# Attention, a leaky-ReLU FFN and a gated FFN in one kernel: the list scheduler's DMA model is given other rates, latencies and a limit on transfers in flight

## The chip, the cores and the metric

The kernel runs on one core of one Trainium2 chip. The metric is the time of one execution in device microseconds (us); the median of three executions stands for a kernel. The engines of the core are PE (TensorE: matmuls, and its weight loads, PEld), DVE (VectorE), ACT (ScalarE), POOL (GpSimd) and SP (SyncE), which here only issues DMAs. Each engine runs its own instructions in program order and waits on semaphores for the others.

## The reference

Three stages follow one another; `x` is what goes from one to the next.

```python
# attention: 4 batches, 8 heads, S = 576, D = 64
scores = q @ k.T / sqrt(64)
cum    = cumsum(log(clip(f, 1e-4, 1)))            # along S, per head
scores = where(causal, -1e9, scores + cum[:, None] - cum[None, :])
attn   = softmax(scores)
x      = (attn @ v)      -> [2304 tokens, 512]
# FFN 1: 512 -> 2048 -> 512
h = x @ w_in;  g = maximum(0.01 * h, h);  x = g @ w_out
# FFN 2: 512 -> 1024 -> 512
h = x @ w2_in; solu = h * softmax(h)
ln = (solu - mean(solu)) / sqrt(var(solu) + 1e-6) * g_ln
out = ln @ w2_out
```

## The kernel before, in words

**Arithmetic.** Where fp32 accuracy is wanted, an operand is split into a high and a low half (a copy, L427/L430/L434, and a subtraction, L442, or L438 where a scale goes with it), and a matmul is three matmuls: high by high, high by low, low by high. So every weight chunk and every block of tokens costs copies and subtractions on ACT, DVE and POOL before PE can use it.

**Attention** goes by 16 pairs of heads. For a pair, pass A does query blocks 0 and 1 and pass B blocks 2 to 4; PASSES (L43) lists eight groups of four pairs, A0, A1, B0, A2, B1, A3, B2, B3 (the figure is the batch). A group needs q and k in SBUF: for pass A `raw<-kqa` and four small rows `raw<-dr_d` that carry the decay, for pass B `raw<-kq`, split into `kq` tiles by copies and subtractions on any of ACT, DVE and POOL; V is loaded as `vr<-vt` and split into `VT`. PE writes scores into `ps_s`, DVE masks them and takes the row maximum (L707), ACT takes the exponential (L657), ACT and DVE scale the result into fp16 halves `hl` (L427, L438), a DMA transpose `pt<-hl` (L470, issued by SP) turns them, PE multiplies by V into `ps_v`, ACT and DVE write that to `xr` (L739, L742), and a DMA spills it to memory: `xs_d<-xr`. There are four `pt` buffers and three `hl` buffers.

**FFN 1, first half.** Nine of the 16 chunks of both weight matrices, wi0 to wi8 and wo0 to wo8, are loaded in 18 transfers of 512 KB each (`wst<-wa`) through three staging buffers, wst0 to wst2. For each, a copy on ACT or POOL makes `wk` from it, DVE shifts bits in place (L812), a copy on ACT, DVE or POOL makes the high half, and a subtraction on POOL or DVE (L442, `wi<-wst,wi` or `wo<-wst,wo`) the low half; then the staging buffer is free for the next transfer. The staging buffers stand in the same memory as the x and g tiles of the FFN, and an operation of no cost frees these only when the last of the 18 is done, so the first FFN matmul waits for all 18. Then the blocks of 256 tokens follow in the order 0, 1, 4, 2, 5, 3, 6, 7, 8 (ORDER), while attention goes on: block 4 is the second block of batch 0 and needs the spill of group B0. A block loads x (`sd<-xs_d`), splits it (`x<-sd`, `x<-sd,x`), multiplies (`ps_f<-x,wi`, "hid" below: 12 matmuls a chunk), applies the leaky ReLU (L853 to L855), multiplies by the second matrix (`ps_f<-g,wo`, "y" below) and spills a partial y to `yp_d`.

**Second phase.** When attention is over, the other seven chunks of both matrices and FFN 2's weights come in through `raw`, and each block of tokens finishes FFN 1 and runs FFN 2 (`ph`, softmax, layer norm, transpose `tr<-hl`, and `py` for the output).

**What sets the order.** Nothing of the above is issued at once. Each piece is recorded as an operation with a duration, a priority, the buffers that it reads and writes and the engines that may do it (class Plan). Plan.run (L161) then plays the program through with a model of the machine: each free engine takes the operation of smallest priority whose inputs have arrived in the model and whose buffers are free in it, and calls its `emit` at that moment. An operation with several engines (flex, L441 to L446 for copies and subtractions) goes to the one where the model sees it done first. So the model's times decide three things and no more: the order of the instructions on each engine, the engine of a flexible operation, and which physical buffer it gets. All DMAs are issued by SP, in the order of the model. In the model a DMA operation is made in move (L462) or turn (L469, transposes), with `dma=` as its time on the transfer engines, which it passes through one after another; in run it has an issue time, a time `ready` at which it may use them, and `end`, at which what depends on it may start. The old model also holds SP during a transpose until the transfer engines are free.

Of the kernel before, what the change touches and what calls it, by code (L numbers as in the profile page):

```python
# [94 lines left out]
WEIGHT2 = {"DVE": 2.58}  # L95
KEPT = {13: (5000.0, -1), 14: (5001.0, -1), 15: (5002.0, -1)}
HEAT = 0.25
TOPE = 267.42
QUEUES = ("SP",)
SHARE = 0.62  # L100
# [11 lines left out]
class Plan:  # L112
# [50 lines left out]
    def run(self):  # L163
# [2 lines left out]
        pool = {e: [] for e in engines}  # L166
        events, cnt = [], 0
        dma_free = hw_free = 0.0
        left = len(self.ops)
        warm, win, busy = False, 0, 0.0  # L170

        def push(t, kind, x):
            nonlocal cnt
            cnt += 1
            heapq.heappush(events, (t, cnt, kind, x))
# [68 lines left out]
        now = 0.0  # L244
        while left:
            moved = True
            while moved:
                moved = False
                for e in engines:
                    if free_at[e] > now or not pool[e]:  # L250
                        continue
                    skipped, got = [], None
                    while pool[e]:
                        item = heapq.heappop(pool[e])
                        o = item[2]
                        if o.taken:
                            continue
                        if o.dma is not None and o.prio > URGENT and dma_free - now > BACKLOG:
                            push(dma_free - BACKLOG + 1.0, 0, None)
                            skipped.append(item)  # L260
                            continue
                        if can_alloc(o) and not (isinstance(o.eng, tuple) and better_elsewhere(o, e)):
                            got = o
                            break
                        skipped.append(item)
                        if len(skipped) > 60:
                            break
                    for item in skipped:
                        heapq.heappush(pool[e], item)
                    if got is None:  # L270
                        continue
                    o = got
                    if isinstance(o.eng, tuple):
                        o.dur, o.eng = cost(o, e), e
                    o.taken = True
                    for b in sorted((b for b in o.bufs if b.slot is None), key=lambda b: b.seq):
                        b.slot = b.tag.free.pop(0)
                        b.t = b.slot() if callable(b.slot) else b.slot
                        b.tag.head += 1
                        bequeath(b.tag)  # L280
                    o.emit()
                    left -= 1
                    moved = True
                    hold = o.dur
                    if e == "PE":
                        hold = pe_time(hold, now, o.heat)
                    elif o.dma is not None and e != "POOL":
                        at = max(now, hw_free)
                        hw_free = at + 460.0
                        hold += at - now  # L290
                    if o.dma is not None:
                        turns = hold >= 1175.0 and e == "SP"
                        ready = (at + (625.0 if turns else 460.0) if e != "POOL" else now + hold) + 650.0
                        s = max(dma_free, ready)
                        if turns:
                            hold += s - ready
                        dma_free = s + o.dma
                        end = dma_free + 1000.0
                    else:
                        end = now + hold + LAT.get(e, 0.0)  # L300
                    free_at[e] = now + hold
                    push(now + hold, 0, None)
                    push(end, 1, o)
                    push(end + TOPE, 2, o)
            if not left:
                break
            assert events, "stuck: " + str([(e, len(p), p[0][:2] if p else None) for e, p in pool.items()])
            now, _, kind, o = heapq.heappop(events)
# [49 lines left out]
def body(tc, kqa, kq, vt, f, wa, w2i, w2o, gln, out):  # L358
    nc = tc.nc
    es = ExitStack()  # L360
    P = Plan()
    PE, ACT, DVE, POOL, SP, CTL = "PE", "ACT", "DVE", "POOL", "SP", "CTL"
# [81 lines left out]
    def flex(engs, durs, emit, prio, **kw):  # L444
        box = []
        o = P.op(tuple(engs) if len(engs) > 1 else engs[0], tuple(durs) if len(engs) > 1 else durs[0],  # L446
                 lambda: emit(box[0].eng), prio, **kw)
        box.append(o)
        return o
# [10 lines left out]
    queue = {SP: nc.sync, ACT: nc.scalar, POOL: nc.gpsimd}  # L460

    def move(dst, src, nbytes, prio, engs=QUEUES, **kw):  # L462
        d = {SP: 475.0, ACT: 490.0, POOL: 1040.0}
        return flex(engs, [d[e] for e in engs], lambda e: queue[e].dma_start(dst(), src()), prio, dma=nbytes / 360.0, **kw)

    def load(buf, dst, src, nbytes, prio, mode="w", **kw):
        return move(dst, src, nbytes, prio, **{mode: [buf]}, **kw)

    def turn(dst, src, n, prio, **kw):  # L469
        return P.op(SP, max(350.0 + 0.875 * n, 1175.0), lambda: nc.sync.dma_start_transpose(out=dst(), in_=src()), prio, dma=0.875 * n, **kw)  # L470

    def mm(o, l, r, start, stop):
        nc.tensor.matmul(o, lhsT=l, rhs=r, start=start, stop=stop)  # L473
# [671 lines left out]
```

## Time and profile before

| | |
|---|---|
| median of 3 executions | 849.26 us (847.44 to 851.11) |
| the profiled execution | 848.65 us |
| its span, first to last instruction | 846.9 us |
| PE busy | 767.9 us, 91% |
| DVE, ACT, POOL busy | 519.4, 490.1, 348.8 us |
| DMA queue of SP | 107.35 MB, 52.3% of the transfer engines' time |

The span leaves 1.75 us of the execution's time outside. The table by stretches (windows) says for each stretch from:to, in us from the span's start, its length, then the busy time of PE, PEld, DVE, ACT and POOL with the instructions in brackets, then the mean granted clock of PE as a share of full speed, the share of the transfer engines' time and the GB/s that they moved. A row of a timeline is one instruction or a run of equal ones: start, length, engine, line, operation, what it writes and from what, shape, count, and in square brackets the idle time before it and what ended that. A row of the waits says which PE instruction waited for which instruction of another engine: total, times, longest.

### The profile page before, as it was taken

What the parts mean: (1) busy time and instruction counts of PE and PEld (TensorE: products, weight loads), DVE (VectorE), ACT (ScalarE), POOL (GpSimd) and SP (SyncE); (2) the same over time, 40 slices, a digit from 0 to 9 for tenths busy, and PEclk for the clock granted to TensorE, in tenths of its full rate; (3) what the DMA queues carried; (4) which work ended last, traced back from release to release, by engine and by line L of the source; (5) the groups of instructions that cost most, each with busy time, mean ns of one, the idle gap of its engine ahead of it and who ended that gap; (6) DMA issues with size and microseconds to landing.
All of it is one profiled execution on the core that took longest, in us unless ns stands there. A gap on an engine that the chain in (4) does not pass through costs nothing.

```text
span 846.9 us, 16019 instructions
## 1 busy us (share of the span) xinstructions
PE 767.9 (91%) x5648; PEld 695.5 (82%) x5648; DVE 519.4 (61%) x1350; ACT 490.1 (58%) x1242; POOL 348.8 (41%) x448
## 2 busy tenths in 40 slices
PE   1753798979999999999899998999999999999996
PEld 1432698968998999999899987898889988998885
DVE  5788767888888878884654667334633434253551
ACT  4886768889889889884555543232333243333321
POOL 6648545166618564822610443422332233222321
PEclk9999999989999999999999999999999999999999
DMA  8997457687789677694655643321332131312223
GB/s 230 220 223 245 96 130 151 150 221 154 136 162 216 155 163 151 174 160 148 195 172 177 189 104 104 71 79 16 98 71 68 26 87 38 87 26 63 26 56 82
DMA packets 184402, 108.37 MB, mean 128 GB/s; under 512 B 150033, under 2 KB 167137, under 8 KB 184321
## 3 DMA queue, kind: packets, MB, share of 16 engines
q1 hardware_dynamic: 184320, 107.35, 52.3%
q8 instruction: 44, 0.72, 0.4%
q14 instruction: 38, 0.30, 0.1%
HBM read 57.39 MB, written 14.78 MB: 85 GB/s over the span
## 4 chain that ended last, share of the span: by engine, by line
PE 64%; DMA 10%; DVE 9%; ACT 8%; issue 4%; POOL 3%; SPq 0%; ACTq 0%; DVEq 0%; POOLq 0%
PE ps_f L473 40%; PE ph L473 10%; PE py L473 6%; PE ps_s L473 5%; PE ps_v L473 3%; ACT ps_s L657 2%; DMA raw<-w2o 2%; DMA tr<-hl 2%; DMA raw<-kq 2%; DMA wst<-wa 1%; DMA pt<-hl 1%; ACT hl L427 1%; DVE hl L438 1%; DMA qa<-sd 1%; DVE ps_s L707 1%
## 5 line engine op out<-in xcount | busy, mean ns | idle before, releaser
L473 PE MATMUL ps_f<-x,wi 128*128 128x256 f32 x972 | 131.7, 289 | 1.2 <-POOL x L442 1.1
L473 PE MATMUL ps_f<-g,wo 128*128 128x256 f32 x972 | 126.4, 284 | 2.5 <-DVE g L855 2.5
L473 PEld LDWEIGHTS ps_f<-x,wi 128*128 128x128 f32 x972 | 124.7, 193 | 3.1 <-POOL x L442 1.9
L473 PEld LDWEIGHTS ps_f<-g,wo 128*128 128x128 f32 x972 | 120.8, 188 | 4.0 <-DVE g L855 2.9
L473 PE MATMUL ph<-wi,g 128*128 128x512 f32 x408 | 98.5, 397 | 1.4 <-DVE raw L968 1.4
L473 PE MATMUL ps_f<-x,wib 128*128 128x256 f32 x756 | 97.3, 279 | 1.8 <-DVE g L855 1.7
L438 DVE SCALAR_TENSOR_TENSOR hl<-ps_s,st,hl 128x512 f16<-128x512 f32 (+4 forms) x160 | 82.8, 540 | 19.4 <-ACT hl L427 16.5
L473 PEld LDWEIGHTS ps_f<-x,wib 128*128 128x128 f32 x756 | 91.6, 188 | 2.9 <-DVE g L855 2.8
L473 PEld LDWEIGHTS ph<-wi,g 128*128 128x128 f32 x408 | 75.9, 188 | 19.3 <-DVE raw L968 1.6
L855 DVE TENSOR_TENSOR g<-ps_f,g 128x256 fp32r<-128x256 f32 x144 | 60.3, 420 | 48.1 <-ACT ps_f L854 47.2
L853 ACT ACTIVATE g<-ps_f 128x256 fp32r<-128x256 f32 x144 | 54.8, 380 | 59.3 <-PE ps_f L473 58.1
L657 ACT ACTIVATE ps_s<-ps_s,st 128x512 f32<-128x512 f32 (+4 forms) x160 | 78.6, 491 | 10.1 <-DVE st L707 6.1
L473 PE MATMUL ps_f<-wo,x 128*128 128x512 f32 x348 | 84.0, 396 | 0.0
L427 ACT ACTIVATE hl<-ps_s,st 128x512 f16<-128x512 f32 (+4 forms) x151 | 76.1, 532 | 11.6 <-DMA pt<-hl 4.7
L473 PE MATMUL ps_v<-pt,VT 128*128 128x128 f16 (+1 forms) x928 | 62.3, 220 | 20.0 <-DVE xr L742 9.0
L473 PE MATMUL py<-g,wob 128*128 128x256 f32 x567 | 75.6, 278 | 2.0 <-ACT g L427 2.0
L473 PEld LDWEIGHTS ps_f<-wo,x 128*128 128x128 f32 x348 | 64.8, 188 | 15.1
L473 PE MATMUL ps_s<-kq 128*128 128x512 f32 (+5 forms) x256 | 66.7, 380 | 11.6 <-DVE hl L438 5.5
L442 POOL TENSOR_TENSOR kq<-raw,kq 64x576 fp32r<-64x576 f32 (+1 forms) x53 | 67.9, 1283 | 21.5 <-ACT kq L427 15.2
L473 PEld LDWEIGHTS <-VT 128*128 128x128 f16 x928 | 50.0, 102 | 30.4 <-issue 15.4
L473 PEld LDWEIGHTS py<-g,wob 128*128 128x128 f32 x567 | 71.2, 188 | 4.3 <-ACT g L427 2.3
L707 DVE CUSTOM_DVE_ANT_0 ps_s<-ps_s,mask 128x256 f32<-128x256 f32 (+3 forms) x128 | 62.2, 496 | 5.9 <-PE ps_s L473 4.5
(159 smaller groups left out, 1221.7 us busy)
## 6 DMA issues: line engine op xcount, KB each, us to landing
wst<-wa SPq DMA_DIRECT2D x18, 512.0 KB
sd<-xs_d SPq DMA_DIRECT2D x32, 256.0 KB
raw<-kq SPq DMA_DIRECT2D x16, 480.0 KB
raw<-wa SPq DMA_DIRECT2D x14, 512.0 KB
raw<-yp_d SPq DMA_DIRECT2D x18, 256.0 KB
vr<-vt SPq DMA_DIRECT2D x13, 320.0 KB
raw<-w2i SPq DMA_DIRECT2D x8, 512.0 KB
raw<-w2o SPq DMA_DIRECT2D x8, 512.0 KB
```

The lines of the kernel that those rows point to most:

```text
L427: nc.scalar.activation(o, i, CP, scale=1.0 if scale is None else scale)
L438: nc.vector.scalar_tensor_tensor(o, a, scale, b, op0=ALU.mult, op1=ALU.subtract)
L442: (nc.vector if eng == DVE else nc.gpsimd).tensor_tensor(o, a, b, op=ALU.subtract)
L473: nc.tensor.matmul(o, lhsT=l, rhs=r, start=start, stop=stop)
L657: P.op(ACT, act(W, 1, True) + 93, lambda view=view, j=j, k=k: nc.scalar.activation(view(), view(), AF.Exp, bias=sts.t[:, j:j + 1], scale=- ...
L707: P.op(DVE, dve(W) + 130, lambda i=i, j=j, view=view: nc.vector.tensor_tensor_reduce(view(), view(), mask[:, 512 - 128 * i:640], -0.125, 3 ...
L853: P.op(ACT, act(n, 0, True), lambda: nc.scalar.activation(g.t[:, 0, 0:n], h(), AF.Prelu, scale=WSC, alpha=0.01), eprio, w=[(g, 0)], r=[ps])
L855: P.op(DVE, dve(n) + 60, lambda: nc.vector.tensor_tensor(g.t[:, 1, 0:n], h(), g.t[:, 0, 0:n].bitcast(F32), op=ALU.subtract), eprio, w=[(g, ...
```

## The change

Only the scheduler's model of DMA differs. A transfer's time in the model goes from its bytes over 360 to its bytes over 267 per ns, so 512 KB take 1.96 us instead of 1.46; a transpose of n columns takes 1.28 n ns instead of 0.875 n. SP is no longer held during a transpose. `ready` is 1300 ns (transposes) or 900 ns after the issue, `end` 700 ns after the transfer, and an issue waits in the model for the landing of the eighth one before it (LANES). The instructions themselves, their shapes and their number of bytes stay; what moves is their order, some choices of engine and some buffers.

```diff
+LANES = 8
@@ run
+        lands = []
@@
-                        at = max(now, hw_free)
+                        at = max(now, hw_free, lands[-LANES] if len(lands) >= LANES else 0.0)
                         hw_free = at + 460.0
                         hold += at - now
                     if o.dma is not None:
-                        turns = hold >= 1175.0 and e == "SP"
-                        ready = (at + (625.0 if turns else 460.0) if e != "POOL" else now + hold) + 650.0
-                        s = max(dma_free, ready)
-                        if turns:
-                            hold += s - ready
-                        dma_free = s + o.dma
-                        end = dma_free + 1000.0
+                        ready = at + (1300.0 if o.dur >= 1175.0 else 900.0) if e != "POOL" else now + hold + 650.0
+                        dma_free = max(dma_free, ready) + o.dma
+                        end = dma_free + 700.0
+                        if e != "POOL":
+                            lands.append(end)
@@ move
-  dma=nbytes / 360.0
+  dma=nbytes / 267.0
@@ turn
-  dma=0.875 * n
+  dma=1.28 * n
```

The first place is SP's queue while the last weights are loaded, before the FFN's first matmul. `pt<-hl` are transposes of group A1, `wst2` is the staging buffer that carries wo4 and then wi8, and `raw0<-kq`, `raw1<-kq` start group B0. Before:

```order
L470 DMA_TRANSPOSE pt1_138<-hl0_134 128x6x128
L470 DMA_TRANSPOSE pt2_139<-hl1_135 128x6x128
L464 DMA wst2_160<-wa 128x2048
L464 DMA wst0_158<-wa 128x2048
L464 DMA raw2_83<-dr_d_104 4x256
L470 DMA_TRANSPOSE pt3_140<-hl2_136 128x6x128
L464 DMA xs_d0_91<-xr1_142 128x256
L464 DMA wst1_159<-wa 128x2048
L464 DMA raw2_83<-dr_d_104 4x256
L464 DMA raw0_81<-kq 128x960
L464 DMA kq1_1_152<-dr_d_104 4x960
L464 DMA raw1_82<-kq 128x960
```

After, from the transpose that stands one ahead of these:

```order
L470 DMA_TRANSPOSE pt0_137<-hl2_136 128x6x128
L464 DMA wst2_160<-wa 128x2048
L464 DMA raw1_82<-dr_d_104 4x256
L470 DMA_TRANSPOSE pt1_138<-hl0_134 128x6x128
L464 DMA xs_d0_91<-xr0_141 128x256
L464 DMA raw1_82<-dr_d_104 4x256 x2
L464 DMA raw2_83<-kqa 64x2x512
L464 DMA wst0_158<-wa 128x2048
L464 DMA raw2_83<-dr_d_104 4x256
L470 DMA_TRANSPOSE pt2_139<-hl1_135 128x6x128
```

The load of wo4 into wst2 moves ahead of two transposes, `pt1<-hl0` and `pt2<-hl1`, and that of wi7 into wst0 ahead of one; a little later, wi8's load into wst2 stands directly behind wo5's into wst1, ahead of both `raw<-kq`, where it was behind them.

The second place is POOL in the same stretch, from wo5's subtraction to wo6's; `kq` are the split q and k of B0's first pairs. Before:

```order
L434 TENSOR_SCALAR kq1_0_151<-raw0_81 64x960
L442 TENSOR_TENSOR kq1_1_152<-raw0_81,kq1_0_151 64x576
L442 TENSOR_TENSOR wo5_77<-wst1_159,wo5_77 128x512
L442 TENSOR_TENSOR kq0_1_150<-raw0_81,kq0_0_149 64x576
L434 TENSOR_SCALAR kq2_0_153<-raw1_82 64x960
L442 TENSOR_TENSOR kq2_1_154<-raw1_82,kq2_0_153 64x576
L442 TENSOR_TENSOR wi8_71<-wst2_160,wi8_71 128x512
```

After:

```order
L442 TENSOR_TENSOR wo5_77<-wst1_159,wo5_77 128x512
L434 TENSOR_SCALAR kq0_0_149<-raw0_81 64x960
L442 TENSOR_TENSOR wi8_71<-wst2_160,wi8_71 128x512
L671 TENSOR_SCALAR st1_129<-st1_129 128x2
L442 TENSOR_TENSOR kq0_1_150<-raw0_81,kq0_0_149 64x576
```

Five pieces of `kq` stood ahead of wi8's subtraction, and one does now; the others come behind it, or go to another engine.

The third place is SP's queue where FFN block 4 is to start: `xs_d0<-xr1` with 320 columns is the last spill of group B0, `sd1` and `sd0<-xs_d0` load block 4's x, and the transposes are those of group A2. Before:

```order
L470 DMA_TRANSPOSE pt1_138<-hl1_135 128x6x128
L464 DMA raw2_83<-kq 128x960
L470 DMA_TRANSPOSE pt2_139<-hl2_136 128x6x128
L470 DMA_TRANSPOSE pt3_140<-hl0_134 128x6x128
L464 DMA yp_d1_96<-yo0_736 128x256
L464 DMA xs_d0_91<-xr1_142 128x320
L464 DMA raw0_81<-kq 128x960
L464 DMA vr0_108<-vt 128x640
L464 DMA yp_d1_96<-yo1_737 128x256
L464 DMA raw1_82<-kq 128x960
L464 DMA sd1_85<-xs_d0_91 128x2x256
L464 DMA sd0_84<-xs_d0_91 128x2x256
```

After:

```order
L464 DMA raw2_83<-kq 128x960
L464 DMA yp_d1_96<-sd2_86 128x256
L464 DMA vr0_108<-vt 128x640
L464 DMA xs_d0_91<-xr1_142 128x320
L470 DMA_TRANSPOSE pt2_139<-hl2_136 128x6x128
L464 DMA raw0_81<-kq 128x960
L470 DMA_TRANSPOSE pt3_140<-hl0_134 128x6x128
L464 DMA yp_d1_96<-yo0_739 128x256
L464 DMA sd1_85<-xs_d0_91 128x2x256
L464 DMA sd0_84<-xs_d0_91 128x2x256
L464 DMA xs_d2_93<-xr0_141 128x256
L464 DMA raw1_82<-kq 128x960
```

The spill stood behind two transposes and a `yp_d` and now stands ahead of them; the loads of x come ahead of `raw1<-kq` and of one `yp_d`. On PE the last matmuls of B0 (`ps_v<-pt,VT`) now have 54 y matmuls of FFN block 1 left behind them, where they had 30.

Elsewhere the same model moves instructions in most of the program. Among the flexible operations, `x<-sd` subtractions on DVE go from 24 to 34 and on POOL from 48 to 38; the copies `kq<-raw` on ACT from 12 to 6 and on POOL from 20 to 26.

## Rows read from the trace of the kernel before

**Rows 1.** The page: span, and busy time, share and instructions by engine.

```profile
span 846.9 us, 16019 instructions
PE 767.9 (91%) x5648; PEld 695.5 (82%) x5648; DVE 519.4 (61%) x1350; ACT 490.1 (58%) x1242; POOL 348.8 (41%) x448
```

**Rows 2.** Stretches of the span (columns as told above).

```profile
64.00:85.00 21.00, 8.07 (x21) 4.84 (x22) 17.94 (x42) 13.71 (x29) 17.11 (x14) 1.00 0.69 238
...
134.00:179.00 45.00, 43.66 (x424) 41.83 (x425) 34.72 (x129) 39.78 (x116) 18.42 (x25) 1.00 0.68 155
179.00:196.00 17.00, 11.10 (x54) 8.29 (x53) 14.94 (x45) 14.83 (x42) 12.97 (x15) 0.70 0.78 219
...
240.00:381.00 141.00, 138.39 (x1287) 130.72 (x1286) 117.33 (x378) 125.85 (x353) 77.38 (x97) 1.00 0.79 170
...
478.00:550.00 72.00, 67.47 (x404) 58.85 (x403) 44.59 (x79) 28.00 (x58) 29.39 (x38) 1.00 0.41 107
550.00:804.00 254.00, 253.32 (x1633) 227.49 (x1632) 107.92 (x207) 85.56 (x190) 73.60 (x109) 1.00 0.24 57
804.00:847.00 43.00, 36.28 (x153) 28.04 (x151) 14.81 (x24) 10.11 (x17) 8.54 (x14) 0.99 0.30 68
```

**Rows 3.** Timeline of PE, around the FFN's first matmuls.

```profile
84.14 0.82 PE L473 MATMUL ps_v<-pt,VT 128*128 128x128 f16 x6 [5.71 <-DVE VT L438]
...
92.41 1.41 PE L473 MATMUL ps_f<-x,wi 128*128 128x256 f32 x5
```

**Rows 4.** Timeline of SP, the loads through wst2 and what is ahead.

```profile
51.06 5.53 SPq L470 DMA_TRANSPOSE pt<-hl  x3
56.69 1.00 SPq L464 DMA_DIRECT2D wst<-wa  x2
...
65.85 0.35 SPq L464 DMA_DIRECT2D wst<-wa  x1
...
79.11 0.33 SPq L464 DMA_DIRECT2D wst<-wa  x1
```

**Rows 5.** Timeline of POOL in the same stretch.

```profile
48.85 1.29 POOL L442 TENSOR_TENSOR wi<-wst,wi 128x512 fp32r<-128x512 f32 x1
...
67.16 1.31 POOL L434 TENSOR_SCALAR kq<-raw 64x960 fp32r<-64x960 f32 x1
...
74.33 1.58 POOL L442 TENSOR_TENSOR kq<-raw,kq 64x576 fp32r<-64x576 f32 x1
77.25 1.83 POOL L442 TENSOR_TENSOR wi<-wst,wi 128x512 fp32r<-128x512 f32 x1 [1.34 <-ACT wi L427]
...
86.55 1.29 POOL L442 TENSOR_TENSOR wo<-wst,wo 128x512 fp32r<-128x512 f32 x1 [1.32 <-ACT wo L427]
```

**Rows 6.** One stretch of 4 us in the same place.

```profile
76.00:80.00 4.00, 2.04 (x5) 0.95 (x3) 3.92 (x9) 3.44 (x9) 2.75 (x2) 1.00 0.32 108
```

**Rows 7.** Timeline of PE: the last matmuls of group B0.

```profile
171.66 0.95 PE L473 MATMUL ps_v<-pt,VT 128*128 128x128 f16 x14
```

**Rows 8.** Timeline of SP, from B0's spill to block 4's x.

```profile
174.13 2.56 SPq L470 DMA_TRANSPOSE pt<-hl  x2
...
177.36 0.44 SPq L464 DMA_DIRECT2D xs_d<-xr  x1
...
180.67 0.96 SPq L464 DMA_DIRECT2D sd<-xs_d  x2
```

**Rows 9.** Timeline of PE: a wait before block 4, and its first matmuls.

```profile
182.98 0.49 PE L473 MATMUL ps_v<-pt,VT 128*128 128x128 f16 x6 [3.53 <-DVE xr L742]
...
189.55 3.35 PE L473 MATMUL ps_f<-x,wi 128*128 128x256 f32 x11 [1.12 <-POOL x L442]
```

**Rows 10.** PE's waits, 196 to 480 us: the longest.

```profile
PE ps_f L473 <- DVE g L855: 2.3, 1, 2.3
```

**Rows 11.** Timeline of DVE: one shape, without and beside POOL's subtraction.

```profile
68.45 0.55 DVE L442 TENSOR_TENSOR kq<-raw,kq 64x384 fp32r<-64x384 f32 x1
...
79.13 1.61 DVE L442 TENSOR_TENSOR kq<-raw,kq 64x384 fp32r<-64x384 f32 x1
```

More of the change, by code (lines that the diff above doesn't have):

```diff
@@ L463, in move @@
         d = {SP: 475.0, ACT: 490.0, POOL: 1040.0}
-        return flex(engs, [d[e] for e in engs], lambda e: queue[e].dma_start(dst(), src()), prio, dma=nbytes / 360.0, **kw)
+        return flex(engs, [d[e] for e in engs], lambda e: queue[e].dma_start(dst(), src()), prio, dma=nbytes / 267.0, **kw)
     def load(buf, dst, src, nbytes, prio, mode="w", **kw):
@@ L469, in turn @@
     def turn(dst, src, n, prio, **kw):
-        return P.op(SP, max(350.0 + 0.875 * n, 1175.0), lambda: nc.sync.dma_start_transpose(out=dst(), in_=src()), prio, dma=0.875 * n, **kw)
+        return P.op(SP, max(350.0 + 0.875 * n, 1175.0), lambda: nc.sync.dma_start_transpose(out=dst(), in_=src()), prio, dma=1.28 * n, **kw)
     def mm(o, l, r, start, stop):
```

## The prediction, made before the changed kernel ran

> **What bounds the kernel now.** I read the page's busy times first. PE works 767.9 us of a span of 846.9 [rows 1], so the whole span holds 79 us in which PE does nothing, and no other engine comes near it. The change alters the order of instructions and some choices of engine; PE's matmuls stay, so the time can move only as those 79 us move, or as the granted clock makes the same matmuls longer.
>
> Second, the table by stretches, to see where they lie [rows 2]. A stretch's length less PE's busy time is its idle time: 5.9 us of 17 in 179 to 196, 4.5 us of 72 in 478 to 550, 6.7 us of 43 at the end, 2.6 us of 141 in 240 to 381, and 0.7 us of 254 in 550 to 804. The greatest part is ahead of the FFN: of 64 to 85 PE works only 8.07 us, and the timeline of PE shows its first FFN matmul at 92.41 [rows 3]. From 134 on PE is full but for a single hole, 179 to 196, and there its granted clock is 0.70 on the mean of the stretch, between the two levels of 2.4 and 1.2 GHz, after PE had little to do.
>
> Third, the timelines around those two places, to see which wait ends last.
>
> **The start.** The first FFN matmul needs all 18 weight chunks through three staging buffers. The loads through wst2 form the chain. Its buffer came free when POOL's subtraction for wi5 ended at 48.85 + 1.29 = 50.14 [rows 5], but SP issued the next load into it, wo4, in the pair at 56.69, since three transposes held SP from 51.06 for 5.53 us [rows 4]. wi8 followed at 65.85 and wo8 at 79.11 [rows 4]. From wo4 to wi8 is 9.2 us, from wi8 to wo8 13.3 us, and from wo8 to the end of its subtraction 86.55 + 1.29 − 79.11 = 8.7 us [rows 4, 5]; 4.6 us later the FFN starts. The middle turn is the long one, because POOL did `kq` pieces from 67.16 to 74.33 + 1.58 = 75.91 and only then wi8's subtraction at 77.25 [rows 5].
>
> **The hole.** The last matmuls of group B0 are issued at 171.66 [rows 7]. Their spill `xs_d<-xr` leaves only at 177.36: two transposes held SP from 174.13 for 2.56 us ahead of it, and block 4's x is loaded at 180.67, 3.3 us after the spill [rows 8]. PE's first full run of matmuls on that x begins at 189.55 [rows 9].
>
> **The change, part by part.** No instruction is removed or added that weighs on PE. The parts of the model (rates, latencies, SP no longer held, eight in flight) act only through one order, so I price the order where PE waits, and not each constant.
>
> *wo4 ahead of two transposes.* One transpose of the three costs SP 5.53 / 3 = 1.84 us [rows 4]. With two behind it and one before, the pair's first load is issued at about 51.06 + 1.84 = 52.9 instead of 56.69: −3.8 us. The two transposes are late by one issue and by one load's time on the transfer engines. Who waits for them? Their products are multiplied by V of group A1, and PE's first matmuls of that kind stand at 84.14, held for 5.71 us by VT and not by the transposes [rows 3]. So this delay is covered by some 25 us; if the cover were gone, it would cost the 3.7 us of two transposes.
>
> *wi8's subtraction ahead of four `kq` pieces.* Five pieces on POOL come to 1.31 + 1.70 + 1.51 + 0.98 + 1.58 = 7.1 us between 67.16 and 75.91 (the first and the last are shown, [rows 5]); one stays ahead. At most 5.8 us go from wi8's turn. But something else is late next: the transfer engines. From 76 to 80 they are busy at 0.32 [rows 6], because there wo8 still waits for its buffer, so 0.68 × 4 = 2.7 us of that stretch stand empty; the page's slices before it show them nearly full. With the loads ahead of it unchanged in bytes, wo8 can move into those 2.7 us and little further, though its buffer would be free 3.8 + 5.8 us earlier. The pieces of `kq` behind wi8 belong to group B0, whose first scores PE does before 84 but whose matmuls by V stand behind block 0's hid in PE's order, so they have cover too.
> Between 2.7 and the 3.8 of wo4's own issue, and since the 0.69 of 64 to 85 [rows 2] leaves a little room more, I take −3.5. At best all idle time of the transfer engines in 64 to 85 goes, 0.31 × 21 = 6.5 us [rows 2]: −6.5. At worst B0's scores or the transposes are late, by the two transposes' 3.7 us: +3.7.
>
> *B0's spill ahead of two transposes.* It leaves 2.56 us earlier for the transposes and some 0.5 for the `yp_d` that it passes, about 3.1 us together [rows 8]; the loads of x keep their 3.3 us of distance. The 24 y matmuls that PE has more behind B0's end (54 for 30) fill the wait from the other side, but that is the same hole, so I count it once: −3. At best the whole hole closes, −5.9 [rows 2]; at worst it doubles, +5.9, which is the rival below. The two transposes are now behind the spill; A2's first matmuls by V in this hole wait 3.53 us for `xr` on DVE [rows 9], not for a transpose, and that is the cover.
>
> *The second phase.* In 478 to 550 the order of `py`, `ph` and hid changes; 4.5 us of idle time are at stake [rows 2]. I see no wait that must go, and take −1, between −3 and +2.
>
> *The end.* The last blocks keep their order and their four output transfers; 6.7 us idle [rows 2] stay: 0.
>
> *New waits.* In 240 to 381 and 550 to 804 PE has 3.3 us idle of 395 [rows 2], so a new order can only lose there. The longest wait from 196 to 480 is 2.3 us [rows 10], and one such wait more, with something small beside it, is +3. The bounds are 0 and another hole of the size of 179 to 196, 5.9, with its clock, 8 in all.
>
> *Engines chosen anew.* Ten more `x<-sd` subtractions go to DVE, off POOL. DVE is busy 34.72 us of 45 in 134 to 179 and POOL 18.42 [rows 2], and the split of x is done ahead of its use, under the matmuls of the block before: 0, and up to a microsecond where block 4 waits for it. DVE's `kq<-raw,kq` of 64x384 took 0.55 us at 68.45 and 1.61 us at 79.13, when POOL's subtraction ran beside it [rows 11]. A rule speaks against the change here: the Trainium skill, page "SBUF — State Buffer", section "SBUF: two separate sides", says that DVE and POOL share a pair of ports as an exclusive lock, and that whichever starts first keeps it for its whole instruction while the other blocks. The trace agrees, with 1.61 for 0.55; by that rule ten moved subtractions cost DVE up to ten times 1.06 us of its own time, which is on PE's path only where DVE is, in the hole.
>
> **Sum.** −3.5 − 3 − 1 + 0 + 3 + 0 = −4.5. The profiled execution took 848.65 us, 1.75 more than its span, so 844.15, with a span near 842.4; it lies 0.6 us under the median of 849.26, so a median of 844.2 to 844.8. I give 844. The bounds add up to −15.4 and +19.6; that all fall on one side is unlikely, and I take 837.5 to 846 for this case.
>
> **The rivals.**
> *No net change, 848.5.* The start is earlier, and it is given back at the hole: from 134 to 179 ACT already works 39.78 us of 45 [rows 2], since attention's exponentials run beside the FFN's ReLU. If the FFN starts 3.5 us earlier and B0's scores do not, block 4 finds its x no earlier, and the hole grows by those 3.5 us. For it: the hole's end is set by attention, not by the FFN. Against it: the spill stood behind transposes for 3 us with its data done. Sum: −3.5 + 3.5 − 3 − 1 + 3 = −1, so 848 to 849.
> *Slower, 855.* Weight loads ahead of transposes and spills ahead of `kq` loads put attention behind: group A2's and B1's scores come later, and a later block of the FFN stands without x as block 4 does. Its place is 179 to 240, its price the hole again: 5.9 us idle, and 11.10 us of matmuls at 0.70 that would take 7.8 at the full clock, 3.3 more [rows 2]. With the start's gain of 3 kept that is +6.2, so 855. It decides if a group's last spill is issued later than 177.36 by over 4 us. For it: ACT has only 5 us to spare in 45, so a delay of attention isn't caught up. By the Trainium skill, page "DMA: Bandwidth & Descriptors", section "Queues, rings and completion order", each DMA engine takes a queue's descriptors in the order of the ring, so a transpose behind a weight load waits for that load; no row here shows the two alone. Against it: in the order, B0's spill moves up, not down.
> *The change doesn't do what it says.* If the order came out nearly alike, the time would stay; it doesn't, since a good half of SP's rows move, so this holds no chance of its own.
>
> **How the numbers follow.** Two runs of this kernel differ by 0.2 to 0.4%, so 0.5%, 4.2 us, is what a measurement can tell from no change: faster means under 845.0, slower over 853.5. A new order over 16019 instructions has many ends that I can't see, so the forecast (844) gets 0.47, no net change (848.5) 0.30, slower (855) 0.23. Faster, same and slower are these same chances. For 8 times in 10 the range runs from 835.5, the start's and the hole's better bounds together (−6.5 − 5.9 − 1) with half of them lost to new waits, to 857, a little above the slower rival; I write 836 to 857, about 1 in 10 at either side.
>
> **What would show it.** Right: the first `ps_f<-x,wi` at 88 to 89 instead of 92.41; POOL's last `wo<-wst,wo` near 82.5; B0's spill within 2 us of its last DVE `xr`; a hole of 3 us or less in place of 5.9, with the clock at 0.8 or more. Wrong: an FFN start at 92 or later (the start's term failed), an idle time in 179 to 196 of 9 us or more (it was given back), or over 5 us of new idle time between 196 and 480 (the new waits were sized too small). A clock under 0.98 over the span would mean that a hole appeared elsewhere.

## The result and the profile after

The changed kernel is slower: 861.22 us, median of 4 (858.86 to 863.62), against 848.99 (847.44 to 851.11); ratio 1.0142, 95% interval 1.0106 to 1.0179. The forecast was 844 and 836 to 857. The profiled execution took 858.86 us with a span of 857.1, 10.2 us more than [rows 1]. It is the fastest of the four, at a granted clock of 0.994; the other three had 0.983 to 0.988, so what follows explains the 10.2 us of this execution and not all of the 12.2 between the medians.

The page of the changed kernel, to be laid beside [rows 1]:

```profile
span 857.1 us, 16028 instructions
...
PE 766.1 (89%) x5648; PEld 696.1 (81%) x5648; DVE 533.0 (62%) x1353; ACT 482.4 (56%) x1230; POOL 345.9 (40%) x456
```

PE does the same 5648 matmuls in 1.8 us less, and idles 91.0 us instead of 79.0. So all of the loss of this execution is idle time of PE, 12.0 us of it. The stretches of the changed kernel, with the columns of [rows 2]:

```profile
0.00:64.00 64.00, 27.34 (x108) 20.58 (x108) 49.17 (x154) 45.38 (x130) 42.52 (x57) 1.00 0.92 234
64.00:106.00 42.00, 25.83 (x140) 22.05 (x141) 32.91 (x83) 29.71 (x69) 25.91 (x28) 1.00 0.50 154
...
134.00:179.00 45.00, 42.35 (x402) 39.50 (x401) 38.00 (x134) 38.02 (x112) 19.71 (x26) 1.00 0.74 161
179.00:196.00 17.00, 11.25 (x72) 9.43 (x71) 14.56 (x42) 13.12 (x39) 12.22 (x16) 0.80 0.73 190
196.00:240.00 44.00, 41.87 (x404) 39.56 (x403) 39.76 (x118) 38.25 (x106) 20.57 (x27) 1.00 0.72 149
240.00:381.00 141.00, 136.31 (x1280) 129.87 (x1279) 117.49 (x364) 124.45 (x348) 76.06 (x94) 1.00 0.74 168
381.00:478.00 97.00, 92.53 (x796) 91.37 (x795) 47.94 (x91) 51.50 (x124) 25.86 (x35) 1.00 0.55 167
478.00:550.00 72.00, 67.26 (x422) 59.66 (x422) 47.36 (x82) 28.75 (x58) 26.29 (x39) 1.00 0.41 110
550.00:804.00 254.00, 249.68 (x1579) 223.05 (x1578) 104.35 (x199) 81.04 (x178) 67.74 (x101) 0.99 0.24 57
```

Four stretches of the kernel before that [rows 2] left out:

```profile
0.00:64.00 64.00, 29.22 (x110) 20.66 (x110) 45.60 (x155) 45.90 (x132) 37.35 (x52) 1.00 0.91 226
64.00:106.00 42.00, 23.76 (x121) 19.50 (x122) 32.64 (x83) 29.53 (x65) 29.07 (x28) 1.00 0.55 168
...
196.00:240.00 44.00, 43.62 (x416) 41.07 (x416) 38.02 (x120) 39.12 (x106) 23.07 (x26) 1.00 0.75 147
...
381.00:478.00 97.00, 94.67 (x822) 94.31 (x821) 50.77 (x90) 52.50 (x123) 28.04 (x34) 1.00 0.57 172
```

The idle time of a stretch is its length less PE's busy time. After minus before, it is +1.9 us up to 64 us, −2.1 in 64 to 106, +1.6 in 106 to 179, −0.1 in 179 to 196, +1.7 in 196 to 240, +2.1 in 240 to 381, +2.1 in 381 to 478, +0.2 in 478 to 550, +3.6 in 550 to 804, and +0.9 behind. There is no single new hole: the loss is many small ones, and behind 196 us none of PE's waits is longer than 1.9 us. Among PE's waits in the changed kernel, two kinds grew most (total, times, longest):

```profile
PE ps_s L473 <- DVE hl L438: 17.7, 10, 4.0
PE ps_f L473 <- DVE g L855: 11.1, 9, 1.8
```

Before, the first stood at 11.5 us and the second at 4.2, in 12 and 6 waits. The second is a run of hid matmuls that waits until DVE has read an earlier hid's PSUM tile.

**The start.** Timelines of the changed kernel: PE's first FFN matmuls, SP's load of wo8 through wst2, POOL's last two subtractions of a weight, DVE's last two shifts of one, and two rows of ACT, a piece of V and its copy of wo8; then two stretches of 4 us.

```profile
90.47 2.91 PE L473 MATMUL ps_f<-x,wi 128*128 128x256 f32 x12
...
70.19 0.33 SPq L464 DMA_DIRECT2D wst<-wa  x1
...
82.30 1.74 POOL L442 TENSOR_TENSOR wo<-wst,wo 128x512 fp32r<-128x512 f32 x1
85.37 1.29 POOL L442 TENSOR_TENSOR wo<-wst,wo 128x512 fp32r<-128x512 f32 x1 [1.33 <-ACT wo L427]
...
80.73 0.68 DVE L812 SCALAR_TENSOR_TENSOR wst<-wst,wk 128x512 int32<-128x512 int32 x1
...
82.81 1.78 DVE L812 SCALAR_TENSOR_TENSOR wst<-wst,wk 128x512 int32<-128x512 int32 x1
...
80.85 0.83 ACT L427 ACTIVATE VT<-vr,vs 128x640 f16<-128x640 f32 x1 [1.08 <-DVE u L631]
81.58 0.76 ACT L427 ACTIVATE wk<-wst 128x512 f16<-128x512 bf16 x1
```

```profile
76.00:80.00 4.00, 1.66 (x4) 0.65 (x3) 3.99 (x11) 3.77 (x9) 2.54 (x3) 1.00 0.25 90
80.00:84.00 4.00, 0.82 (x6) 0.66 (x7) 3.60 (x9) 1.69 (x3) 2.36 (x2) 1.00 0.03 4
```

wo8 is issued at 70.19 instead of 79.11 [rows 4], 8.9 us earlier, yet POOL's last subtraction starts at 85.37 instead of 86.55 [rows 5] and the FFN at 90.47 instead of 92.41 [rows 3]. From 80 to 84 the transfer engines are empty (0.03): the data is there and waits. ACT's copy of wo8 starts only at 81.58, behind the piece of V that waited 1.08 us for DVE. DVE is busy for 3.99 of 4 us in 76 to 80, among others with a piece of `kq` of a shape that POOL did there before, and its last shift of a weight comes at 82.81. The kernel before has the same rows 1.2 to 1.3 us later, on ACT and on DVE:

```profile
82.11 0.83 ACT L427 ACTIVATE VT<-vr,vs 128x640 f16<-128x640 f32 x1 [1.48 <-DVE u L631]
82.85 0.76 ACT L427 ACTIVATE wk<-wst 128x512 f16<-128x512 bf16 x1
...
84.00 1.78 DVE L812 SCALAR_TENSOR_TENSOR wst<-wst,wk 128x512 int32<-128x512 int32 x1
```

There DVE was as full, 3.92 of 4 us [rows 6]. So wo8's chain waited for ACT and DVE, whose earlier work had moved by little more than a microsecond. The last shift takes 1.78 us, the one before it 0.68, and POOL's subtraction runs beside it from 82.30 for 1.74. The Trainium skill, page "SBUF — State Buffer", section "SBUF: two separate sides", says that the later of the two blocks until the other's instruction is over; the trace agrees, with 1.1 us lost here. It is no loss of the change, since the shift took 1.78 us before as well.

**The hole.** SP, PE and DVE of the changed kernel in 165 to 196:

```profile
171.38 0.45 SPq L464 DMA_DIRECT2D xs_d<-xr  x1
...
177.06 0.95 SPq L464 DMA_DIRECT2D sd<-xs_d  x2
```

```profile
185.29 1.01 PE L473 MATMUL ps_s<-kq 128*128 128x384 f32 x2 [3.97 <-DVE hl L438]
187.97 2.07 PE L473 MATMUL ps_s<-kq 128*128 128x512 f32 x4 [1.67 <-DVE st L671]
189.84 2.41 PE L473 MATMUL ps_f<-x,wi 128*128 128x256 f32 x12
```

```profile
185.16 2.36 DVE L442 TENSOR_TENSOR x<-sd,x 128x256 fp32r<-128x256 f32 x2
187.44 0.47 DVE L438 SCALAR_TENSOR_TENSOR hl<-ps_s,st,hl 128x256 f16<-128x256 f32 x1
187.84 0.14 DVE L671 TENSOR_SCALAR st<-st 128x1 f32<-128x1 f32 x1
```

The spill leaves 6.0 us and the loads of x 3.6 us earlier than in [rows 8], and block 4 starts at 189.84, as before at 189.55 [rows 9]. PE now waits 3.97 and 1.67 us for attention's softmax on DVE, with the y matmuls of block 1 used up. Before, the longest wait of the hole was one for attention's `xr` on DVE too, 3.53 us, and only 1.12 us were for block 4's x [rows 9]. In the changed kernel two subtractions of that x stand on DVE for 2.36 us directly ahead of the softmax piece that ends PE's second wait; before, DVE did one of the four and POOL three. The hole has 5.75 us instead of 5.90.

### The profile page after: what moved, and what is told of

It reads as the page before. It is cut to its first block, busy times and chain, and to the rows that moved or that the text cites. A ratio compares the mean times of both kernels' runs of the same rounds, so it can differ in the third digit from the quotient of the medians.

```text
span 857.1 us, 16028 instructions
## 1 busy us (share of the span) xinstructions
PE 766.1 (89%) x5648; PEld 696.1 (81%) x5648; DVE 533.0 (62%) x1353; ACT 482.4 (56%) x1230; POOL 345.9 (40%) x456
## 4 chain that ended last, share of the span: by engine, by line
PE 51%; DMA 6%; DVE 4%; ACT 2%; issue 2%; POOL 2%; SPq 0%; DVEq 0%; ACTq 0%; POOLq 0%
PE ps_f L473 30%; PE ph L473 10%; PE py L473 6%; PE ps_s L473 3%; DMA tr<-hl 3%; PE ps_v L473 2%; DMA raw<-wa 2%; DMA sd<-xs_d 1%; ACT raw L962 1%; POOL hl L442 1%; DVE raw L968 1%; DVE s L960 1%; DVE g L442 1%; DVE g L855 0%; ACT wk L427 0%
## 5 line engine op out<-in xcount | busy, mean ns | idle before, releaser
L473 PE MATMUL ps_f<-wo,x 128*128 128x512 f32 x336 | 81.5, 398 | 0.6 <-ACT x L427 0.6
L473 PEld LDWEIGHTS ps_f<-wo,x 128*128 128x128 f32 x336 | 62.7, 189 | 15.8 <-ACT x L427 1.4
L473 PEld LDWEIGHTS ps_s<-kq 128*128 128x128 f32 (+1 forms) x256 | 42.2, 200 | 27.8 <-DVE hl L438 11.8
```

## The experiments

Theory A: the order before is a picked one, and any reordering loses, whatever moves it. Theory B: one part of the new model is at fault. Theory C: the new model is the worse one as such. Every kernel below computes the same; only the scheduler's model differs. "us of the model's time" are those of the scheduler's own clock, in which the second phase begins at 388.4.

All of them stand in one table: the ratio to before with its interval, PE's idle time by stretch in us (from one profiled execution each; before has 53.0, 9.2, 4.9, 4.5, 0.7 and 6.6) and PE's busy time (before 767.9), which rises where the granted clock was lower. The six columns of idle time and the busy time add up to the span of the profiled execution, which need not be the median one.

| kernel | ratio | 0–106 | 106–240 | 240–478 | 478–550 | 550–804 | rest | busy |
|---|---|---|---|---|---|---|---|---|
| changed | 1.0142 (1.0106–1.0179) | 52.8 | 12.4 | 9.2 | 4.7 | 4.3 | 7.6 | 766.1 |
| j990 | 1.0204 (1.018–1.0228) | 51.3 | 9.8 | 14.9 | 2.0 | 0.7 | 6.7 | 773.8 |
| j361 | 1.0116 (1.0073–1.0158) | 50.4 | 7.6 | 12.0 | 1.2 | 0.4 | 6.8 | 771.7 |
| j1010 | 1.0045 (1.0023–1.0067) | 50.3 | 11.1 | 9.4 | 1.8 | 0.4 | 6.5 | 767.7 |
| a690 | 1.0098 (1.0069–1.0126) | 53.6 | 12.2 | 7.3 | 0.9 | 4.5 | 8.2 | 766.1 |
| a268 | 1.0197 (1.017–1.0224) | 53.4 | 14.1 | 5.6 | 5.3 | 4.6 | 7.6 | 772.0 |
| rates | 1.0373 (1.0349–1.0397) | 60.3 | 9.6 | 15.3 | 5.3 | 4.7 | 7.8 | 775.5 |
| lat | 1.0076 (1.0061–1.0092) | 49.1 | 6.5 | 10.6 | 4.6 | 0.5 | 8.3 | 769.6 |
| lanes | 1.0281 (1.0254–1.0309) | 51.6 | 13.9 | 13.1 | 7.6 | 0.8 | 6.7 | 775.6 |
| old_then_new388 | 1.0039 (1.0013–1.0066) | 53.3 | 8.7 | 4.5 | 1.5 | 4.8 | 7.6 | 773.5 |
| new_then_old388 | 1.0101 (1.0071–1.0131) | 53.2 | 12.4 | 9.0 | 5.7 | 0.7 | 6.6 | 767.1 |
| old_then_new200 | 1.0078 (1.005–1.0107) | 52.8 | 9.1 | 6.3 | 1.5 | 4.9 | 7.6 | 769.7 |
| old_then_990 | 0.9994 (0.9973–1.0015) | 52.9 | 8.1 | 6.7 | 3.8 | 0.6 | 6.7 | 770.5 |
| p2_turn | 1.0131 (1.0102–1.016) | 51.6 | 7.8 | 4.8 | 6.0 | 4.0 | 7.9 | 776.9 |
| p2_move | 1.0052 (1.0032–1.0071) | 52.5 | 8.0 | 4.4 | 5.1 | 1.0 | 7.7 | 772.9 |
| after_turn | 1.0081 (1.0056–1.0105) | 53.6 | 12.9 | 9.1 | 4.3 | 0.7 | 7.9 | 765.7 |
| lat200 | 1.003 (1.0018–1.0043) | 50.0 | 7.2 | 9.2 | 5.5 | 0.4 | 6.5 | 769.6 |
| lat180 | 0.9988 (0.9966–1.0009) | 52.5 | 5.8 | 7.1 | 4.2 | 0.7 | 6.4 | 770.2 |
| lat160 | 0.9957 (0.9935–0.9978) | 48.2 | 5.3 | 5.6 | 4.3 | 0.4 | 6.5 | 770.7 |

Some of these kernels repeat another one's order up to a point, so the table shows how far two executions of one order differ. Up to 478 us PE's order is one and the same in before, old_then_new388, p2_turn and p2_move, and another one in the changed kernel, new_then_old388 and after_turn. Their idle time in 240 to 478 is 4.4 to 4.9 us in the first four and 9.0 to 9.2 in the other three; in 106 to 240 it is 7.8 to 9.2 and 12.4 to 12.9. So the changed kernel's loss there belongs to its order, while a difference under 2 us in the first two columns says little by itself.

**1. A hair's change of the old model** (j990, j361, j1010).

```diff
-                        end = dma_free + 1000.0
+                        end = dma_free + 990.0     # j990; 1010.0 in j1010
-  dma=nbytes / 360.0
+  dma=nbytes / 361.0                               # j361
```

j990: 

> The kernel before with one figure of its model moved by a hair: what depends on a DMA may start 990 ns after the transfer instead of 1000. As a model of the machine it is as good as before. Theory A (before is a picked order: any reordering loses, whatever moved it): 853 to 866 us, ratio to before 1.005 to 1.02, with PE's added idle time spread over many places as in the changed kernel. Theory B (one part of the new model is at fault): within 0.5% of before, 845 to 853.

j361: 

> The kernel before with a transfer's time in the model as bytes over 361 instead of 360 per ns. Theory A: 853 to 866 us. Theory B: 845 to 853. Theory C (the new model is the worse one as such, beyond the reordering): between before and the changed kernel, nearer to before, 846 to 855.

j1010: 

> The kernel before with 1010 ns instead of 1000, the other side of the first run. Theory A: 1.005 to 1.03 of before, with another place for the new idle time than the run with 990. If the loss with 990 had to do with a DMA's latency in the model being too small, the other side would gain or stay: 0.99 to 1.003.

All three lose, by 2.0, 1.2 and 0.45%, and the first loses more than the change under study. Ten nanoseconds in one latency of the model change PE's order from its 546th matmul on, at 140 us. The idle time grows in 240 to 478 us, where the order before has 4.9 us and these have 14.9, 12.0 and 9.4. A had named another place for j1010 than for j990, and 1.005 at least; neither came. Only in j990 does the idle time of the whole span grow by more than half a microsecond, by 6.4 us, beside 5.9 us more of PE's busy time. j361 idles 78.3 us in all for before's 79.0: its profiled execution lost 3.8 us of busy time, at a granted clock of 0.91 in 106 to 179. The profiled execution of j1010 lost next to nothing (span 847.1 for 846.9), and its 0.45% shows only in the medians. So it is shown that the three are slower, and not that they lose their time in one common place.

Two stretches of j990:

```profile
240.00:381.00 141.00, 132.82 (x1214) 125.99 (x1212) 120.58 (x359) 118.78 (x334) 73.94 (x90) 0.98 0.74 162
381.00:478.00 97.00, 90.25 (x772) 88.30 (x771) 50.34 (x103) 53.08 (x129) 22.09 (x29) 0.98 0.53 161
```

So B in its plain form falls: a reordering that means nothing costs as much as the change.

**2. One part alone** (rates, lat, lanes).

```diff
# rates: only move / 267.0 and turn 1.28 * n
# lat: only ready = at + 1300 or 900, end = dma_free + 700, SP not held
# lanes: only at = max(now, hw_free, lands[-8])
```

rates: 

> Only the rates are changed (bytes over 267, 1.28 n); latencies, SP's hold and the issue as before. Theory A: 853 to 866 us, no nearer to before than a hair's change. Theory B, rates at fault: 857 to 865; rates not at fault: 845 to 853.

lat: 

> Only the latencies are changed (ready 1300 or 900 ns after the issue, end 700 ns after the transfer, SP not held by transposes). Theory A: 853 to 866 us. Theory B, latencies at fault: 857 to 865; not at fault: 845 to 853.

lanes: 

> Only the limit of eight transfers in flight is added, rates and latencies as before. Theory A: 1.005 to 1.04 of before. Theory B, the limit at fault: 1.012 to 1.02 with rates and latencies near 1; but rates alone gave 1.037 and latencies alone 1.008, so B in its plain form can no longer hold, whatever comes out here.

The parts don't add up: they cost 3.7, 0.8 and 2.8% alone and 1.4% together. rates went past what A named for it (878.74 us), and lat, with 852.44 us, stayed under A's 853. A's "any reordering" holds for the sign, not as a spread that all share.

**3. A hair's change of the new model** (a690, a268).

```diff
-                        end = dma_free + 700.0
+                        end = dma_free + 690.0     # a690
-  dma=nbytes / 267.0
+  dma=nbytes / 268.0                               # a268
```

a690: 

> The changed kernel with one figure moved by a hair: end 690 ns after the transfer instead of 700. Theory A, and the new model neither better nor worse: within the spread of the old model's neighbours, 1.005 to 1.03 of before, so 850 to 871 at this chip's 846, and as likely to be faster than the changed kernel as slower. Theory C (the new model is the worse one): 1.015 or more, slower than both of the old model's neighbours (1.020 and 1.012) on the mean.

a268: 

> The changed kernel with bytes over 268 instead of 267 per ns in the model. Theory A: 1.005 to 1.03 of before. Theory C: 1.015 or more. If the new model were the better one and the changed kernel only an unlucky draw of it: under 1.01.

They lose 1.0% and 2.0%: the new model's three draws (with the changed kernel) have a mean of 1.0146, the old model's three neighbours one of 1.0122. That doesn't tell them apart, and a690 alone lies under C's 1.015. But one column does: 550 to 804 has 4.3 to 4.6 us idle in all three of the new and 0.4 to 0.7 in all of the old. In experiment 2 it has 4.7 us with the new rates alone, and 0.5 and 0.8 with the latencies or the limit.

**4. Cut at a time** (the old model up to a time of the model's clock, then the new, and the reverse). A cut leaves every instruction ahead of it where it was.

```diff
+  fresh = (now >= SWITCH) == AFTER      # 388.4 us or 200 us
+  if fresh: (new ready, dma_free, end, limit) else: (the old)
# old_then_990:  end = dma_free + (1000.0 if now < 200000.0 else 990.0)
```

old_then_new388: 

> The old model up to 388.4 us of the model's own time, where the second phase begins (some 460 us on the chip), the new one from there: every instruction up to there stands in the order of the kernel before. Of the 12 us of idle time that the changed kernel added, 7.4 lay ahead of 550 us and 4.7 behind. Theory A, with each stretch a draw of its own: idle time ahead of 460 as before within 0.5 us, and 0 to 5 us more behind, ratio 1.000 to 1.006. If the new model is bad for the second phase as such (a transpose or weight load that it times wrongly): +4 to +6, ratio 1.005 to 1.007, with the same waits for DVE g and ACT wib as in the changed kernel.

new_then_old388: 

> The other way round: the changed kernel's order up to the second phase, then the old model. Theory A: it keeps the 7.4 us of the first part and draws the second anew, +7 to +12, ratio 1.008 to 1.014. If the second phase was at fault, +3 to +8, with the end of the span free of what the changed kernel added there.

old_then_new200: 

> The old model up to 200 us of the model's time (some 240 on the chip), the new one from there: the start and the hole at 179 to 196 are those of the kernel before. Theory A: the idle time up to 235 us is that of before, and 240 to 478 loses 3 to 8 us of the advantage that the order before has there (4.9 us idle against 9 to 15 in all others so far); ratio 1.003 to 1.015. Theory of the hole (the loss is carried over from the earlier start of the FFN): no loss behind 240, ratio 0.997 to 1.003.

old_then_990: 

> The old model throughout, but from 200 us of its time a DMA's end is 990 ns after the transfer instead of 1000. The control for the run with the new model from there. Theory A: no better than that one, ratio 1.003 to 1.015 with the added idle time behind 240. If the new model is the worse one as such: under 1.003, and the run with the new model at least 0.5% above it.

550 to 804 in the first two, whose first parts are those of the other kernel each:

```profile
550.00:804.00 254.00, 249.19 (x1581) 222.85 (x1580) 107.61 (x204) 81.31 (x180) 69.01 (x102) 0.99 0.24 59
```

```profile
550.00:804.00 254.00, 253.33 (x1629) 227.29 (x1628) 104.78 (x203) 84.00 (x186) 73.67 (x107) 1.00 0.25 60
```

The first is old_then_new388 and idles 4.8 us, the second new_then_old388 with 0.7. So this loss comes with the new model in the second phase, whatever stands ahead: C holds there. By time old_then_new388 lies in A's range and under C's (1.0039 for 1.005 to 1.007), since 478 to 550 gained 3.1 us. And old_then_990 lost nothing (0.9994), against A: where the first 240 us are those of before, what follows need not lose, and 240 to 478 took 6.7 us, not the 9 to 15 of the full draws. old_then_new200 lost 0.8%, with 6.3 us there and 4.9 in 550 to 804, so what was written down for C, a control under 1.003 and the new model 0.5% above it, came true in this one pair.

**5. Which constant in the second phase** (p2_turn, p2_move, after_turn).

```diff
# p2_turn, from 388.4 us on, on the kernel before
-  dma_free = s + o.dma
+  dma_free = s + o.dma * (1.28 / 0.875 if now >= 388400.0 and o.dur >= 1175.0 else 1.0)
# p2_move: the same with 360 / 267 for all but transposes
# after_turn: the changed kernel, transposes times 0.875 / 1.28 from 388.4 us on
```

p2_turn: 

> The kernel before with the transposes' time in the model at 1.28 n instead of 0.875 n from the second phase on, and nothing else. If the transposes' rate is the cause: 4 to 5 us idle in 550 to 804 with two waits of 1.8 us for DVE g, the tail 1 us longer, ratio 1.003 to 1.007. If the other transfers' rate is the cause, or only the two together: 0.4 to 1 us idle there, ratio 0.997 to 1.002.

p2_move: 

> The kernel before with the other transfers' bytes over 267 instead of 360 from the second phase on, transposes as before. If the transposes' rate is the cause: 0.4 to 1 us idle in 550 to 804, ratio 0.997 to 1.002. If this rate is the cause: 4 to 5 us there, 1.003 to 1.007.

after_turn: 

> The changed kernel with the transposes' time in the model back at 0.875 n from the second phase on (388.4 us of the model's time); every instruction ahead of that as in the changed kernel. If the transposes' rate is needed for the loss of the second phase: 0.4 to 1 us idle in 550 to 804 instead of 4.3, no wait of 1.8 us for DVE g there, ratio to before 1.007 to 1.012 for the changed kernel's 1.014. If the latencies or the other rate bring it as well: 3 us or more there and 1.012 to 1.017.

The stretch 550 to 804 of p2_turn, of p2_move and of after_turn:

```profile
550.00:804.00 254.00, 249.98 (x1575) 223.93 (x1574) 101.72 (x195) 84.50 (x186) 67.07 (x96) 0.99 0.23 57
```

```profile
550.00:804.00 254.00, 253.03 (x1615) 226.41 (x1614) 105.44 (x207) 87.67 (x194) 72.46 (x106) 1.00 0.24 59
```

```profile
550.00:804.00 254.00, 253.31 (x1631) 227.50 (x1630) 104.93 (x203) 82.45 (x184) 75.85 (x112) 1.00 0.25 59
```

The transposes' rate brings the 4 us (4.0 in p2_turn, 1.0 in p2_move, 0.7 before), and taking it out of the changed kernel removes them (0.7 for 4.3), with the ratio going from 1.0142 to 1.0081. It is two waits that come and go. PE's waits for DVE's g in 550 to 804, in the changed kernel, as in p2_turn, and in after_turn, as before:

```profile
PE ps_f L473 <- DVE g L855: 3.5, 2, 1.8
```

```profile
PE ps_f L473 <- DVE g L855: 0.6, 2, 0.4
```

The first of the two, in the changed kernel, then in after_turn:

```profile
622.57 2.98 PE L473 MATMUL ps_f<-x,wib 128*128 128x256 f32 x24
627.32 1.90 PE L473 MATMUL ps_f<-x,wib 128*128 128x256 f32 x12 [1.77 <-DVE g L855]
```

```profile
624.37 1.57 PE L473 MATMUL ps_f<-x,wib 128*128 128x256 f32 x12
625.77 1.20 PE L473 MATMUL py<-g,wob 128*128 128x256 f32 x9
...
627.15 1.55 PE L473 MATMUL ps_f<-x,wib 128*128 128x256 f32 x12
629.12 1.66 PE L473 MATMUL ps_f<-x,wib 128*128 128x256 f32 x12 [0.43 <-DVE g L855]
```

Three hids in a row (24 and 12 matmuls) outrun ACT and DVE, which empty their PSUM tiles (the kernel has three `ps_f`), and the third waits 1.77 us; with the y matmuls (9, and 3 in the row left out) between the first and the second, it waits 0.43. The other wait of 1.77 us stands at 714.97 in the changed kernel. Why a longer transpose in the model lets the y matmuls fall behind was not followed up.

By time both kernels of the old model missed. p2_turn lost 1.3%, not the 0.3 to 0.7% expected: its profile has 3.0 us more idle time and 9.0 us more PE busy time than before, at granted clocks of 0.60 in 179 to 196 and 0.96 behind 804. Of the 9.0 us, 3.9 lie in its first 3836 matmuls, which stand in the order of before, so that share is not the model's; what lowered the clock stays open. p2_move lost 0.5%, where 0.997 to 1.002 was expected if the transposes' rate is the cause and 1.003 to 1.007 if the other transfers' rate is; its profile has 0.4 us less idle time and 5.0 us more busy time than before, at granted clocks of 0.54 in 179 to 196 and 0.95 in 478 to 550. So the idle time of the stretch tells the two rates apart, and the time doesn't.

**6. The best first part** (lat200, lat180, lat160): the new latencies alone up to 200, 180 or 160 us of the model's time, then the old model.

```diff
+  fresh = now < 160000.0
+  if fresh: ready = at + 1300 or 900; end = dma_free + 700; SP not held
+  else: (the old)
```

lat200: 

> The new latencies alone up to 200 us of the model's time (some 240 on the chip), then the old model. Idle time up to 235 us as in the kernel with the new latencies throughout, 56 us for 62, the second phase as before (12 us), so all hangs on 240 to 478: with the 5 us of the order before the time would be 6 us under before (0.993), with the 9 to 15 of the old model's neighbours 2 us under to 4 over (0.998 to 1.005). I take 0.999.

lat180: 

> The same with the switch at 180 us of the model's time, a second draw of what follows: 0.993 to 1.005. If the two differ by over 0.5% with the same first 210 us, what follows is set by the draw and not by what the start hands on.

lat160: 

> The new latencies alone up to 160 us of the model's time (some 190 on the chip), then the old model: a third draw. If the earlier start is worth what its idle time says, 56 us for 62 up to 235, the mean over the draws lies under 1 and this one at 0.993 to 0.999; if what follows takes it back each time, 0.999 to 1.006, as the first two (1.003 and 0.999).

lat160 beats both kernels: 844.0 us, 0.9957 (0.9935 to 0.9978). It is the best of three draws (1.003, 0.9988, 0.9957, mean 0.9992), so the start alone is not shown to be worth 0.4%. Its stretches around the hole and where the other draws lose:

```profile
179.00:196.00 17.00, 16.64 (x152) 14.82 (x150) 14.15 (x43) 15.02 (x40) 10.85 (x14) 1.00 0.94 183
...
240.00:381.00 141.00, 135.72 (x1263) 128.17 (x1264) 116.80 (x340) 114.62 (x321) 74.58 (x89) 1.00 0.74 159
381.00:478.00 97.00, 96.67 (x797) 95.63 (x796) 56.12 (x95) 51.18 (x120) 30.72 (x37) 1.00 0.61 189
```

The hole is gone: 0.4 us idle at full clock. SP loads block 4's x here at 156.89 already, 24 us ahead of [rows 8], with attention further along (PE has done 322 `ps_v` matmuls by 179 us, and 292 before):

```profile
156.89 1.08 SPq L470 DMA_DIRECT2D sd<-xs_d  x2
```

## Why the prediction was wrong, step by step

**The start, −3.5.** The chain through wst2 moved as told and more, 8.9 us at wo8 for the 2.7 to 3.8 that I allowed. The FFN began 1.9 us earlier, at 90.47 instead of my 88 to 89. The step "something else is late next: the transfer engines" named the wrong one. It was DVE, and ACT behind it, with DVE nearly full from 72 to 80, as it had been before: the row from which I read the transfer engines' 0.32 has 3.92 of 4 us for DVE [rows 6]. The reading of POOL as the cause was wrong too: in [rows 5] POOL idles 1.34 us ahead of wi8's subtraction and 1.32 ahead of wo8's, each time until ACT's copy. PE's idle time fell by 2.1 us in 64 to 106, and rose by 1.9 in the first 64 us, which I had not priced. The three traces of the changed order have 36.6 to 36.7 us idle there, and the six of the order before 34.3 to 35.0.

**The hole, −3.** The spill moved 6.0 us, and the idle time by −0.1. The spill did leave earlier, as priced and by more, 0.2 us behind the last `xr` of DVE ahead of it; but it was not what ended most of the hole. [rows 9] said so: 3.53 us of it were a wait for attention's `xr`, and 1.12 for block 4's x. The first rival said "the hole's end is set by attention", and for this place it holds; lat160, with attention further along, is the case where the hole closes. I had costed the engines chosen anew at 0 from the busy times of 134 to 179. Two subtractions of x now stand on DVE in the hole, ahead of the softmax that PE waits for; no run took them out, so their price stays open.

**The second phase, −1.** The idle time in 478 to 550 went up by 0.2 us.

**New waits, +3.** This is the term that decided, and the step that failed: +1.6 in 106 to 179, +1.7 in 196 to 240, +4.2 in 240 to 478 and +3.6 in 550 to 804, 11.2 us together, and 9.6 of them behind 196 us, beyond its bound of 8. My own sign of it, over 5 us between 196 and 480, came true with 6.0. I sized it by the longest single wait of the kernel before. But its rows said something else: 3.3 us idle in 395 us is little room to gain and much to lose, and I now think that the number of places where a fresh order can lose, not the longest loss, sets the size; that is argued, not shown. Of the 11.2 us, 3.6 belong to the transposes' rate, shown by putting it in and by taking it out. The rest is not tied to a constant: neighbours of the old model that differ by 10 ns idle 4.5 and 10 us more in 240 to 478 alone, though j1010 gains nearly as much elsewhere.

**The end, 0.** It cost 0.9 us in the changed kernel. The structure stayed; the last blocks' waits for `wib` on ACT grew from 1.1 to 2.8 us.

**The rivals.** The slower one had the sign and, at 855, half the size, but its mechanism was not what happened: no spill came later, no hole doubled, and no clock was lost (0.994 for 0.993 in the profiled executions). No rival said "many small waits".

**The sums.** The worse bounds come to +20.6 with the microsecond that I named for the engines chosen anew, not +19.6. And 835.5 is close to all of the −13.4, though I wrote that half of it was lost to new waits. Neither of the two sets the 857 that the measured time went past.

## What to carry to other kernels

When a change touches the numbers that a scheduler plays with, price it as a new draw of the whole order before pricing any place: look for the stretches where the critical engine idles 1 or 2%, and expect the loss there. Read the whole row, too: the engine that is full in it is the next limit, whichever column you came for. A control with a meaningless change of the same numbers costs one run, and tells whether there is a cause to look for at all. A cut, with the old model up to a time and the new one behind it, separates the parts that such a draw mixes, and its first part is a second trace of an order that is already known.

## What was not expected

A model changed by 10 ns in one latency made the kernel 2.0% slower, and another by 0.3% in one rate 1.2%: the order of 16000 instructions is that sensitive, and a difference of 1% between two models says little by itself.

A short stop costs clock. Stretches of 5 us of the changed kernel around the hole:

```profile
180.00:185.00 5.00, 1.32 (x13) 0.87 (x11) 4.29 (x17) 4.89 (x15) 4.27 (x8) 0.98 1.16 297
185.00:190.00 5.00, 3.04 (x7) 2.15 (x8) 4.84 (x9) 3.54 (x11) 4.46 (x4) 0.50 0.65 167
```

PE works 1.32 of 5 us, and the granted clock of the next 5 us is 0.50, the lower of its two levels.
